# A clustered-attention and feed-forward kernel: the last unit's two output tiles in two PSUM places, copied in halves by two engines, and another list of priority shifts

## The chip, the cores and the metric

The kernel runs on one core of one Trainium2 chip. The metric is the device time of one execution in microseconds. The kernel before takes 863.71 us, the median of 3 runs (863.14 to 864.28).

## The reference: what is computed

Sizes: 4 batches, 8 heads, 768 positions, head width 64; 16 clusters; a feed-forward net of 512 to 2048 to 512 on 3072 tokens. Cut to what matters:

```python
q_assign = argmax(einsum('bhsd,hcd->bhsc', q_n, c_n), -1)   # q_n, k_n, c_n: normalised rows
k_assign = argmax(einsum('bhsd,hcd->bhsc', k_n, c_n), -1)
scores = where(q_assign[..., :, None] == k_assign[..., None, :], q @ k.T / sqrt(D), -1e9)
attn = exp(scores - max) / sum
x = (attn @ v).transpose(0, 2, 1, 3).reshape(3072, 512)
h = x @ w_in                                   # 512 -> 2048
g = where(h >= 1, h, where(h <= -1, 0, (h + 1)**2 / 4))
out = g @ w_out                                # 2048 -> 512
```

Every position gets the label of the nearest centroid; attention runs only between equal labels; its result goes through the two-layer net.

## The kernel before

**The units.** The work is cut into 12 units u, one for each batch and each third of its 768 query positions (256 queries, `CQ`). A unit has four pairs of heads. For each pair come four score steps (`at_scores`): TensorE (PE) multiplies keys with queries into a PSUM place of two banks, `pair[0]` (page name `pair<-kv,q`), and VectorE (DVE) drains it with a custom operation into one of three SBUF buffers `sS`, with the row statistic in `sbi`; this drain is the operation that lets PE write the next scores. ScalarE (ACT) takes the exponential, ACT and GpSimd (POOL) split it into a high and a low f16 half (`hl`), and SyncE (SP) sends it through a transposing DMA (`pT<-hl`). `at_av` multiplies the transposed weights with the values into bank `banka`, and the result goes by way of `rb` to `x`. The labels of a batch's queries come from a small product with the centroids (`bankj<-cT,q`), whose operand `q` is a transposing DMA of the normalised queries `qn`.

**The net.** For each unit and each f of eight slices of the hidden width, `ffn1` does 24 matmuls into one of the banks `bankh`, `banki`, `bankj`; DVE, ACT and POOL make the activation `r` and its two halves `g`. `ffn2` then does 12 matmuls (`pair<-w,g`, 128x512) that add to `pair[1]`, which has two banks: one for each of the unit's two output tiles t (128 queries x 512). After the last f of a unit, ACT copies both tiles, with a scale, to the SBUF tile `o` (`o<-pair,f_io`, 128x512 each), and one DMA writes them out. For the last unit and the last f (`end`) the 12 matmuls come as six for tile 0 and then six for tile 1, and each tile has a DMA of its own. So `pair[0]` serves scores, `pair[1]` the output; in the first 22 steps (`EARLY`) scores use both in turn.

**The first 120 us** also load and prepare the weights (`w`, `wk`, `word`: operations of DVE, ACT and POOL on 128x1024 tiles), the queries and the keys of the first batch.

**What sets the order.** No engine instruction is issued where it stands in the code: `Recorder` records each with what it reads and writes. `issue` then plans: 59 passes (`BASE`) of list scheduling, forward and backward, with a price for each instruction; then each seed of the list `NUDGES` calls `nudge`, which draws from the seed some events (a run of neighbouring names, or every second or fifth) and shifts their priority by a random amount; and a last forward pass fixes one order for every engine. Line 350 of the kernel before, in `issue`, replays the recorded calls; so nearly all rows of the profile say L350, and the names of the tiles tell operations apart. An engine runs its own list strictly in order. `Recorder` also keeps two engines from touching the same PSUM bank at the same time.

Of the kernel before, what the change touches and what calls it, by code (L numbers as in the profile page):

```python
# [11 lines left out]
F32 = mybir.dt.float32  # L12
U32 = mybir.dt.uint32
AF = mybir.ActivationFunctionType
ALU = mybir.AluOpType
# [27 lines left out]
LOOK, MARGIN = 0.4, 4000  # L43
BASE = 59
NUDGES = (
# [25 lines left out]
)  # L71
TILED = 248

# [386 lines left out]
def view(buf, shape, dtype):  # L460
    n = 1
    for k in shape:
        n *= k
    ap = buf.bitcast(dtype)[:, :n]
    if len(shape) > 1:
        names = "abcd"[: len(shape)]
        ap = ap.rearrange(
            "p (" + " ".join(names) + ") -> p " + " ".join(names), **dict(zip(names[1:], shape[1:]))
        )
    return ap  # L470
# [3 lines left out]
def tile_clustered_attention_moe(  # L474
# [14 lines left out]
    DM, DFF = w_in.shape  # L489
# [5 lines left out]
    CT = 2  # L495
# [3 lines left out]
    NU = B * NCH  # L499
# [15 lines left out]
    rec = Recorder(tc)  # L515
# [7 lines left out]
    def new(tag, shape, dtype, n=1):  # L523

        if tag not in rings:
            size = mybir.dt.size(dtype)
            for k in shape:
                size *= k
            rings[tag] = Ring(tiles(tag, n, -(-size // 32) * 32))
        return rings[tag](*shape, dtype=dtype)  # L530
# [23 lines left out]
    pair = [psum.tile([P, 1024], F32, name=f"pair{i}") for i in range(2)]  # L554
# [617 lines left out]
    F = {}  # L1172
# [27 lines left out]
    def ffn2(u, f):  # L1200
        b, c = divmod(u, NCH)
        e = FS[u, f]
        g = F.pop((u, f))
        if e["first"]:
            F[u] = view(pair[1], [CT, DM], F32)
        po = F[u]
        terms = [(s, i, *x) for s in range(2) for i, x in enumerate(((0, 0), (0, 1), (1, 0)))]
        end = u == NU - 1 and f == NF - 1

        parts = [(terms, [t]) for t in range(CT)] if end else [(terms[:3], range(CT)), (terms[3:], range(CT))]  # L1210
        for part, ts in parts:
            with rec.group():
                for s, i, ga, wa in part:
                    for t in ts:
                        rec.tensor.matmul(
                            po[:, t],
                            g[:, ga, s * CQ + t * P : s * CQ + (t + 1) * P],
                            w2[f][:, wa, s, :],
                            start=(e["first"] and s == 0 and i == 0),
                            stop=(e["last"] and s == 1 and i == 2),  # L1220
                        )
        if e["last"]:
            fresh = (u, "o") not in F
            if fresh:
                F[u, "o"] = new("o", [CT, DM], F32)
            ob = F[u, "o"]
            for t in range(CT):
                if fresh:
                    rec.scalar.activation(out=ob[:, t], in_=po[:, t], func=AF.Copy, scale=e["io"])
                else:  # L1230
                    rec.vector.scalar_tensor_tensor(
                        out=ob[:, t], in0=po[:, t], scalar=e["io"], in1=ob[:, t], op0=ALU.mult, op1=ALU.add
                    )
        if f == NF - 1:
            to = out.rearrange("(b p t) e -> b p t e", b=B, t=T)[b, :, c * CT : (c + 1) * CT, :]
            for part in [slice(t, t + 1) for t in range(CT)] if end else [slice(0, CT)]:
                rec.sync.dma_start(to[:, part], ob[:, part])
# [14 lines left out]
    for b in range(B):  # L1252
# [11 lines left out]
        for c in range(NCH):  # L1264
            u = b * NCH + c
            s0 = first(b, 0, c)
            for x, fn in zip((PRO, -9.1, -8.1, -6.1) if u == 0 else (s0 - 14, s0 - 6.8, s0 - 6.4, s0 - 4.5), (q_load, q_scale, q_split, q_assign)):
                at(x, fn, u)
            for hp in range(0, NP, NP if c else 1):
                at(first(b, hp, c) - (5.5 if u == 0 else 3), q_pairs, u, hp, NP if c else 1)  # L1270
            for hp in range(NP):
                s0 = first(b, hp, c)
                for n in range(SC):
                    at(s0 + n, at_scores, b, hp, c, n // CT, n % CT)
                    at(s0 + n + 1, at_soft, b, hp, c, n // CT, n % CT)
                at(s0 + LA - 0.5, at_av, b, hp, c)

            sf = max(sf, s0 + FA)
            G = NF if u else GF
            for f in range(NF):  # L1280
                if f % G == 0 and (u < 2 or c == 0):
                    if u == 0:
                        sf = max(sf, wat[2 * (f + G) - 1] + 2)
                    at(sf - 1, ffn_scale, [u] if u == 0 else range(u, (b + 1) * NCH), range(f, f + G))
                at(sf, ffn1, u, f)
                at(sf + 3, ffn2, u, f)
                sf += 2
# [50 lines left out]
```

## Time and profile before

| | |
|---|---|
| time, median of 3 runs | 863.71 us |
| the profiled execution's own time | 860.89 us |
| its span, first to last instruction | 859.1 us |
| mean granted TensorE clock | 0.985 |
| busy: PE, DVE, ACT, POOL | 802.4, 652.3, 639.1, 548.3 us |
| DMA | 142.53 MB, mean 166 GB/s |

The profile is one execution. Its span lacks 1.8 us that lie around the first and the last instruction, and it is 2.8 us below the median of the runs. Rows of groups give busy time, the mean of one instruction, and the idle time of the engine just before them with what ended it; rows of a timeline give start, length, engine, line, operation, tiles and count, and in brackets the idle time before and its releaser. PE's rows overlap a little, because matmuls are pipelined.

### The profile page before, as it was taken

How to read it: one execution, taken by the hardware profiler on the slowest of the kernel's cores; microseconds unless marked ns; L12 is line 12 of the kernel's file. 1: busy time of each engine (PE TensorE's matmuls, PEld its weight loads, DVE VectorE, ACT ScalarE, POOL GpSimd, SP SyncE). 2: the span in 40 equal slices, each digit the busy share in tenths (PEclk: the TensorE clock that was granted, in tenths of full speed). 3: DMA queues.
4: the chain of work that ended last, by engine and by line, in shares of the span. 5: the costliest groups of instructions: out<-in, count | busy, mean ns of one | idle time of the engine just before them, and what ended most of it. 6: DMA issues, size and time to landing. Idle time of an engine off the chain costs nothing.

```text
span 859.1 us, 19058 instructions
## 1 busy us (share of the span) xinstructions
PE 802.4 (93%) x7148; PEld 555.1 (65%) x7148; DVE 652.3 (76%) x1507; ACT 639.1 (74%) x1128; POOL 548.3 (64%) x527
## 2 busy tenths in 40 slices
PE   3677669999999999999999999999999999999997
PEld 2555446576666776767676766766676767676664
DVE  7999999989977877678888768678888767544322
ACT  6889898897877787687776787786876686776232
POOL 1156887887666768676766678656667567766221
PEclk9989899999999999999999999999999999999999
DMA  9975799889999989999898989997998696755100
GB/s 305 253 218 136 231 208 193 161 156 195 208 167 166 191 144 175 192 183 181 174 223 137 176 149 174 195 188 172 188 181 165 124 174 122 121 124 114 20 26 25
DMA packets 404766, 142.53 MB, mean 166 GB/s; under 512 B 372800, under 2 KB 396352, under 8 KB 404672
## 3 DMA queue, kind: packets, MB, share of 16 engines
q1 hardware_dynamic: 404672, 141.30, 81.7%
q8 instruction: 56, 0.92, 0.4%
q14 instruction: 38, 0.31, 0.1%
HBM read 40.40 MB, written 6.29 MB: 54 GB/s over the span
## 4 chain that ended last, share of the span: by engine, by line
PE 71%; DVE 9%; issue 3%; ACT 3%; POOL 3%; DMA 2%; ACTq 0%; DVEq 0%; POOLq 0%
PE pair L350 35%; PE banka L350 10%; PE banki L350 9%; PE bankj L350 9%; PE bankh L350 8%; DVE sS L350 2%; DVE r L350 2%; DMA q<-qn 1%; POOL hl L350 1%; ACT sS L350 1%; DVE qn L350 1%; DMA pT<-hl 1%; ACT hl L350 1%; DVE w L350 1%; DVE banki L350 0%
## 5 line engine op out<-in xcount | busy, mean ns | idle before, releaser
L350 POOL TENSOR_TENSOR hl<-sS,hl 128x768 f16<-128x768 f32 x176 | 297.4, 1695 | 109.6 <-ACT hl L350 90.4
L350 PE MATMUL pair<-w,g 128*128 128x512 f16 x1152 | 272.9, 380 | 0.7 <-ACT o L350 0.7
L350 PEld LDWEIGHTS <-w 128*128 128x128 f16 x2304 | 223.9, 98 | 50.3 <-issue 5.7
L350 ACT ACTIVATE sS<-sS,sbi 128x768 f32<-128x768 f32 x192 | 179.2, 933 | 86.7 <-DVE sbi L350 80.6
L350 DVE CUSTOM_DVE_ANT_0 sS<-pair,zero,er 128x768 f32<-128x768 f32 x192 | 193.8, 1011 | 48.3 <-PE pair L350 43.2
L350 PEld LDWEIGHTS <-g 128*128 128x128 f16 x1152 | 110.8, 98 | 116.1 <-issue 3.6
L350 PE MATMUL pair<-kv,q 128*128 128x384 f16 x768 | 158.3, 329 | 17.1 <-ACT pT L350 8.5
L350 POOL TENSOR_TENSOR g<-r,g 128x512 f16<-128x512 f32 x88 | 106.4, 1209 | 74.3 <-ACT g L350 64.1
L350 ACT CAST hl<-sS 128x768 f16<-128x768 f32 x176 | 144.0, 825 | 9.7 <-DMA pT<-hl 6.6
L350 PEld LDWEIGHTS <-q 128*128 128x128 f16 x992 | 78.7, 98 | 72.3 <-issue 25.5
L350 PE MATMUL banka<-pT,kv 128*64 128x256 f16 (+1 forms) x1680 | 106.3, 280 | 0.2 <-DMA pT<-hl 0.2
L350 ACT ACTIVATE r<-r,f_ra,f_rs 128x512 f32<-128x512 f32 x88 | 71.2, 809 | 37.5 <-DVE r L350 35.1
L350 PEld LDWEIGHTS <-kv 128*64 128x64 f16 (+1 forms) x1824 | 92.4, 108 | 4.0 <-ACT kv L350 1.4
L350 ACT CAST g<-r 128x512 f16<-128x512 f32 x88 | 53.8, 612 | 16.9 <-DVE r L350 8.0
L350 PE MATMUL bankj<-x,w 128*128 128x256 f16 x408 | 48.6, 272 | 3.4 <-POOL x L350 1.8
L350 PE MATMUL bankh<-x,w 128*128 128x256 f16 x432 | 51.8, 273 | 0.0
L350 POOL TENSOR_TENSOR qn<-qn,phi 128x256 f16<-128x256 f16 x48 | 33.0, 704 | 16.1 <-DVE phi L350 11.0
L350 POOL TENSOR_TENSOR w<-w 128x1024 f16<-128x1024 f32 x12 | 28.8, 2409 | 16.1 <-ACT w L350 16.1
L350 PE MATMUL banki<-x,w 128*128 128x256 f16 x312 | 37.7, 273 | 0.1
L350 PE MATMUL banki<-wk,w 128*128 128x256 f16 x312 | 37.4, 273 | 0.0
L350 ACT ACTIVATION_READ_ACCUMULATOR sS<-sS,sbi 128x1 f32 x192 | 36.0, 187 | 0.0
L350 DVE TENSOR_SCALAR r<-bankh,f_lo,f_hi 128x512 f32<-128x512 f32 x30 | 24.2, 805 | 13.7 <-PE bankh L350 10.9
(252 smaller groups left out, 1068.0 us busy)
## 6 DMA issues: line engine op xcount, KB each, us to landing
w<-in_moe_w_out_dram SPq DMA_DIRECT2D x14, 512.0 KB, 5.2
q<-in_q_dram SPq DMA_DIRECT2D x12, 512.0 KB, 4.7
kv<-in_k_dram SPq DMA_DIRECT2D x16, 384.0 KB, 4.3
kv<-in_v_dram SPq DMA_DIRECT2D x16, 384.0 KB, 4.1
out_dram<-o SPq DMA_DIRECT2D x11, 512.0 KB, 3.4
w<-in_moe_w_in_dram SPq DMA_DIRECT2D x10, 512.0 KB, 6.9
word<-in_moe_w_in_dram SPq DMA_DIRECT2D x6, 512.0 KB, 4.6
o<-in_v_dram SPq DMA_DIRECT2D x8, 384.0 KB, 3.9
```

The lines of the kernel that those rows point to most:

```text
L350: fn(*args, **kw)
```

## The change

`ffn2` holds a unit's output as a list of two views instead of one. For units 0 to 10 these are the two banks of `pair[1]` as before. For the last unit, tile 1 goes to the first bank of `pair[0]`. At the end of the last unit each tile is copied in two halves, columns 0 to 255 by ACT and columns 256 to 511 by DVE, where one ACT instruction copied 512 columns. And `NUDGES` is another list: 158 seeds from 1650000017 to 1650094381 stand for 194 seeds from 1700000017 to 1700116959. The rules of `nudge` are the same. The seeds are arguments to a hash, so their values say nothing to a reader; one line of each list is shown.

```diff
 NUDGES = (
-    1700000017, 1700000018, 1700000028, 1700000071, 1700000073, 1700000079, 1700000104, 1700000109,
...
+    1650000017, 1650000027, 1650000052, 1650000066, 1650000181, 1650000212, 1650000275, 1650000278,
...
         if e["first"]:
-            F[u] = view(pair[1], [CT, DM], F32)
+            F[u] = [pair[1][:, t * DM : (t + 1) * DM] for t in range(CT)]
+            if u == NU - 1:
+                F[u][1] = pair[0][:, :DM]
         po = F[u]
...
                         rec.tensor.matmul(
-                            po[:, t],
+                            po[t],
...
             for t in range(CT):
-                if fresh:
-                    rec.scalar.activation(out=ob[:, t], in_=po[:, t], func=AF.Copy, scale=e["io"])
+                if end:
+                    half = DM // 2
+                    rec.scalar.activation(out=ob[:, t, :half], in_=po[t][:, :half], func=AF.Copy, scale=e["io"])
+                    rec.vector.tensor_scalar(
+                        out=ob[:, t, half:], in0=po[t][:, half:], scalar1=e["io"], scalar2=None, op0=ALU.mult
+                    )
+                elif fresh:
+                    rec.scalar.activation(out=ob[:, t], in_=po[t], func=AF.Copy, scale=e["io"])
```

PE, ACT, POOL and SP have as many recorded instructions as before; DVE has two more, the two halves. The orders are the same but for small swaps up to about 100 us of the profile before; from there on all five differ. Three places follow. Numbers behind the names tell buffers apart (`pair0_79` is `pair[0]`).

**The end, ACT and DVE.** The last rows of ACT before, with the semaphores that they wait for:

```order
L350 ACTIVATE hl1_172<-hl1_172,f_ra0_194,f_rs0_199 128x512 [waits DVE_49]
L350 CAST g1_76<-hl1_172 128x512 [waits DVE_49,PE_49,Pool_49]
L350 ACTIVATE o0_68<-pair1_80,f_io0_189 128x512 [waits DMAHW0_49,PE_49]
L350 ACTIVATE o0_68<-pair1_80,f_io0_189 128x512
L1333 UNCONDITIONAL_BRANCH
```

The last rows of ACT now:

```order
L345 ACTIVATE hl1_172<-hl1_172,f_ra0_194,f_rs0_199 128x512 [waits DVE_49]
L345 CAST g1_76<-hl1_172 128x512 [waits DVE_49,PE_49,Pool_49]
L345 ACTIVATE o0_68<-pair1_80,f_io0_189 128x256 [waits DMAHW0_49,PE_49]
L345 ACTIVATE o0_68<-pair0_79,f_io0_189 128x256 [waits PE_49]
L1336 UNCONDITIONAL_BRANCH
```

The last rows of DVE now:

```order
L345 SCALAR_TENSOR_TENSOR hl0_171<-banki_83,f_gs0_204,hl0_171 128x512 [waits Activation_49]
L345 TENSOR_SCALAR hl1_172<-bankj_84,f_lo0_184,f_hi0_179 128x512 [waits PE_49,Pool_49]
L345 SCALAR_TENSOR_TENSOR hl1_172<-bankj_84,f_gs0_204,hl1_172 128x512 [waits Activation_49]
L345 TENSOR_SCALAR o0_68<-pair1_80,f_io0_189 128x256 [waits DMAHW0_49,Activation_49]
L345 TENSOR_SCALAR o0_68<-pair0_79,f_io0_189 128x256 [waits Activation_49]
L1336 UNCONDITIONAL_BRANCH
```

ACT's two copies are half as wide and each has a wait for PE of its own; DVE's halves stand at the end of its list and wait for ACT, not for PE: a tile's two halves follow one another. SP's two output DMAs wait for DVE now, for ACT before.

**PE behind the preparation of the last weights (about 116 to 124 us of the profile before).** PE before; `wk,ones` is part of the weight preparation, `kv1,q1` and `kv2,q1` are scores of unit 1, `w0,g0` is ffn2 of unit 0, `idu,rr` and `pT,kv` belong to `at_av`; repeats are left out:

```order
L350 MATMUL bankj_84<-aq0_126,ones_113 128x4
...
L350 MATMUL bankh_82<-wk0_69,ones_113 128x128
...
L350 MATMUL pair0_79<-kv1_62,q1_66 128x384
...
L350 MATMUL pair1_80<-w0_78,g0_75 128x512
...
L350 MATMUL banka_81<-idu_93,rr1_168 64x128
...
L350 MATMUL banka_81<-pT2_166,kv0_61 64x256
```

PE now:

```order
L345 MATMUL bankj_84<-aq0_126,ones_113 128x4
...
L345 MATMUL bankh_82<-wk0_69,ones_113 128x128
...
L345 MATMUL pair0_79<-kv1_62,q1_66 128x384
...
L345 MATMUL pair0_79<-kv2_63,q1_66 128x384
...
L345 MATMUL banka_81<-idu_93,rr1_168 64x128
...
L345 MATMUL banka_81<-pT2_166,kv0_61 64x256
```

Six ffn2 matmuls that stood between a score group and `at_av` have moved to behind the `at_av` group, and the next score group stands in their place, directly behind the score that uses the same PSUM place.

**DVE, the rescaling of the queries of batch 1 for the next head pair (about 136 to 141 us).** `ISA` is the drain of the scores. DVE before:

```order
L350 ISA sS0_85,sbi2_158<-pair0_79,zero_111,er1_148 128x768
L350 ISA sbi2_158 128x1
L350 TENSOR_REDUCE v_am1_125<-x2_74 128x1
L350 TENSOR_TENSOR banki_83<-zs0_145,mx0_146 128x16x16
L350 ISA sS1_86,sbi3_159<-pair0_79,zero_111,er1_148 128x768
L350 ISA sbi3_159 128x1
L350 TENSOR_TENSOR banki_83<-banki_83,iota_94 128x16x16
L350 TENSOR_REDUCE mx0_146<-banki_83 128x16
L350 TENSOR_TENSOR zs0_145<-banki_83,mx0_146 128x256
L350 TENSOR_SCALAR q1_66<-q1_66,phi0_149 128x512
```

DVE now:

```order
L345 ISA sS0_85,sbi2_158<-pair0_79,zero_111,er1_148 128x768
L345 ISA sbi2_158 128x1
L345 TENSOR_SCALAR q1_66<-q1_66,phi0_149 128x512
L345 TENSOR_REDUCE zs0_145<-banki_83 128x256
L345 SCALAR_TENSOR_TENSOR r0_209<-bankh_82,f_gs0_204,r0_209 128x512
L345 TENSOR_REDUCE mx0_146<-zs0_145 128x16
L345 ISA sS1_86,sbi3_159<-pair0_79,zero_111,er1_148 128x768
```

The rescaling `q1<-q1,phi` stood behind the drain into `sbi3` and three operations more; it now stands ahead of that drain.

Further on, on PE: the ffn1 group that starts at 157.85 us before now has an `at_av` group of 36 matmuls ahead of it; the ffn2 group that starts at 165.09 us has 33 matmuls between it and the `at_av` group ahead of it, where 16 stood, and ACT's two copies of unit 0's tiles to `o`, which had three operations between them, now follow each other directly behind the copy `rb<-banka` of that `at_av` group; and the label group `bankj<-cT,q` of unit 3, which stood between an `at_av` group and a score, now stands between two score groups, with nothing else between these.

More of the change, by code (lines that the diff above doesn't have):

```diff
@@ L1227, in ffn2 @@
             for t in range(CT):
-                if fresh:
-                    rec.scalar.activation(out=ob[:, t], in_=po[:, t], func=AF.Copy, scale=e["io"])
+                if end:
[6 more added lines that the diff above has]
+                    rec.scalar.activation(out=ob[:, t], in_=po[t], func=AF.Copy, scale=e["io"])
                 else:
                     rec.vector.scalar_tensor_tensor(
-                        out=ob[:, t], in0=po[:, t], scalar=e["io"], in1=ob[:, t], op0=ALU.mult, op1=ALU.add
+                        out=ob[:, t], in0=po[t], scalar=e["io"], in1=ob[:, t], op0=ALU.mult, op1=ALU.add
                     )
```

43 rows, old and new, of the table NUDGES are left out of this document.

## The prediction

> **What bounds the kernel now.** I read the page first (busy times, the slices, the chain), then the windows, then PE's waits, then the timeline at each of them.
>
> ```profile
> PE 802.4 (93%) x7148; PEld 555.1 (65%) x7148; DVE 652.3 (76%) x1507; ACT 639.1 (74%) x1128; POOL 548.3 (64%) x527
> ...
> PE   3677669999999999999999999999999999999997
> DVE  7999999989977877678888768678888767544322
> PEclk9989899999999999999999999999999999999999
> ...
> PE 71%; DVE 9%; issue 3%; ACT 3%; POOL 3%; DMA 2%; ACTq 0%; DVEq 0%; POOLq 0%
> ```
>
> PE carries 93% of the span and 71% of the chain that ended last. The slices show where it is not full: the first six, about 120 us, in which DVE has the 9s. The windows put numbers to that:
>
> ```profile
> 20.00:120.00 100.00, 69.07 (x616) 49.47 (x612) 97.97 (x233) 91.24 (x139) 58.74 (x45) 0.90 0.79 213
> ...
> 0.00:120.00 120.00, 74.67 (x705) 54.38 (x706) 112.47 (x277) 103.94 (x159) 61.88 (x72) 0.91 0.81 227
> 120.00:854.60 734.60, 727.75 (x6444) 500.71 (x6442) 539.79 (x1231) 533.85 (x968) 486.39 (x456) 1.00 0.83 156
> ```
>
> From 20 to 120 us DVE is busy for 97.97 of 100 us; up to 120 us PE idles 120 − 74.67 = 45.33 us. Behind that PE idles only 734.60 − 727.75 = 6.85 us in 734.6, at a granted clock of 1.00. The change leaves every PE instruction as it is, so from 120 us on an order can win at most these 6.85 us, and what lies behind the last matmul. PE's waits from 120 us on name them:
>
> ```profile
> PE pair L350 <- DVE sbi L350: 4.1, 4, 2.9
> PE bankj L350 <- DMA q<-qn: 1.2, 2, 1.0
> PE bankj L350 <- DVE r L350: 1.0, 2, 0.6
> PE pair L350 <- DVE q L350: 0.8, 1, 0.8
> PE bankj L350 <- DVE has L350: 0.8, 1, 0.8
> PE pair L350 <- ACT o L350: 0.7, 1, 0.7
> PE bankj L350 <- DVE f_rs L350: 0.6, 1, 0.6
> PE banka L350 <- DMA pT<-hl: 0.2, 1, 0.2
> ```
>
> They sum to 9.4 us; the longest, 2.9, ends at 119.74 us and lies ahead of the window, so 6.5 us of 6.85 are named. A measurement of this kernel can tell about 0.2%, 1.7 us, from no change: a quarter of that budget.
>
> **The end.** Last matmuls, ACT's two copies, the two DMAs; then the rows that price a half.
>
> ```profile
> 851.62 2.97 PE L350 MATMUL pair<-w,g 128*128 128x512 f16 x13
> 854.63 1.26 ACT L350 ACTIVATE o<-pair,f_io 128x512 f32<-128x512 f32 x2 [4.53 <-PE pair L350]
> 855.35 0.91 SPq L350 DMA_DIRECT2D out_dram<-o  x2
> ...
> L350 ACT ACTIVATE o<-pair,f_io x24: 665/679/687, 162.1 to 855.2; 128x512 f32<-128x512 f32 x24
> ...
> L350 PE MATMUL pair<-w,g 128*128 128x512 f16 x1152 | 272.9, 380 | 0.7 <-ACT o L350 0.7
> ...
> L350 ACT CAST g<-r 128x512 f16<-128x512 f32 x88 | 53.8, 612 | 16.9 <-DVE r L350 8.0
> ...
> L350 ACT COPY rb<-banka x48: 345/360/374, 54.4 to 802.5; 128x256 f32<-128x256 f32 x48
> L350 DVE TENSOR_TENSOR rb<-banka,rb x44: 393/419/426, 133.8 to 802.9; 128x256 f32<-128x256 f32 x44
> ...
> L350 ACT CAST x<-rb x24: 387/402/441, 58.9 to 685.0; 128x256 f16<-128x256 f32 x24
> ...
> out_dram<-o SPq DMA_DIRECT2D x2, 256.0 KB, 2.1
> ```
>
> PE ends at 854.59 and both copies lie behind that, though tile 0's six matmuls are over 6 x (2.97 − 0.38)/12 = 1.3 us earlier: the copy of tile 0 waits for all of the tile `pair[1]`. They end at 854.63 + 1.26 = 855.89. With tile 1 in `pair[0]`, tile 0 is copied from about 853.3, beside tile 1's matmuls, and its DMA leaves at about 854.3. Behind PE stands one tile. ACT's half: a cast is 612 ns at 512 columns and 402 at 256, 0.21 less, so 0.68 − 0.21 = 0.47 us; DVE's half 0.42 (`rb<-banka,rb`, as wide, out of PSUM too), estimates both. The order lets DVE wait for ACT, so they add: 854.63 + 0.47 + 0.04 + 0.45 = 855.59, or −0.30. The first DMA, now 1 us ahead, leaves the second more of the 2.1 us that they share: 0 to −0.2. I take −0.45; the bounds are −0.3 and, if the halves lay side by side, −0.95.
>
> On that I weighed the Trainium skill: its page "PSUM — Partial Sum Buffer", section "PSUM bank collisions raise a hardware error", says that two engines must not touch one bank in the same quadrant at the same time. By it the cut into halves can bring no overlap, only the shorter second operation; no run here shows two engines in one bank at once.
>
> **The new order, up to 120 us.** DVE sets this stretch, its work is the same and stands there in the same order but for swaps of single operations. A swap moves a drain by one operation, such as the 0.80 us of an `r` (first row below), and back again. I take 0, bounds −0.8 and +0.8.
>
> **The new order, 119 to 127 us.**
>
> ```profile
> L350 DVE TENSOR_SCALAR r<-bankh,f_lo,f_hi 128x512 f32<-128x512 f32 x30 | 24.2, 805 | 13.7 <-PE bankh L350 10.9
> ...
> 119.74 1.44 PE L350 MATMUL pair<-kv,q 128*128 128x384 f16 x4 [2.90 <-DVE sbi L350]
> 120.97 2.44 PE L350 MATMUL pair<-w,g 128*128 128x512 f16 x6
> ...
> 124.05 2.15 PE L350 MATMUL banka<-pT,kv 128*64 128x256 f16 x35 [0.19 <-DMA pT<-hl]
> ...
> 126.60 1.46 PE L350 MATMUL pair<-w,g 128*128 128x512 f16 x6
> ...
> 121.98 1.00 DVE L350 CUSTOM_DVE_ANT_0 sS<-pair,zero,er 128x768 f32<-128x768 f32 x1
> 122.92 0.08 DVE L350 DVE_READ_ACCUMULATOR2_ANT sbi<- 128x1 f32 x1
> ```
>
> Before, six ffn2 matmuls fill the time from the score at 119.74 until `pT` lands at 124.05; at that place they take 2.44 us where the same six take 1.46 at 126.60, so PE runs at about half speed behind its wait of 2.90 us, and at full speed again in the `at_av` row. Now a score stands in their place and must wait until the score before is drained, by this row until about 123.0, less 0.7 as one such `r` has left DVE's list ahead of it: 122.3. PE then idles about 1.2 us, does the score and is ready for `at_av` by about 123.9 (0.25 us of transposes included), when `pT` lands anyway. What is lost is that 2.44 us of slow ffn2 are left for later, where they take 1.3 (1.46 less the overlap of its last matmul), while a score of 0.65 to 1.2 us is done already. With a clock that is full again by then, 1.3 − 0.65 less what goes of the 0.19 and of the slow work: +0.35. With a clock that stays at half through the `at_av` group, whose 2.15 us become 4.3, +2.5. I take +1.0, nearer the first, since the idle time is shorter than the 2.90 that went with the slow rows.
>
> The Trainium skill, "TensorE: Matmul & The Clock Gate", Part 1, says that the clock falls to half after an idle window of about 3.4 us and is full again after a busy one; by that rule a new idle stretch inside the slow window would keep it slow, which is the slower case below. The rows agree on the half speed (1.44 us for a score here).
>
> **The new order, 127 to 167 us.**
>
> ```profile
> 133.94 0.81 PE L350 MATMUL pair<-kv,q 128*128 128x384 f16 x4 [0.20 <-DVE sbi L350]
> ...
> 141.53 0.82 PE L350 MATMUL pair<-kv,q 128*128 128x384 f16 x4 [0.82 <-DVE q L350]
> ...
> 157.85 1.47 PE L350 MATMUL bankj<-x,w 128*128 128x256 f16 x12 [0.64 <-DVE f_rs L350]
> ...
> 165.09 1.46 PE L350 MATMUL pair<-w,g 128*128 128x512 f16 x6 [0.75 <-ACT o L350]
> ```
>
> Four waits, 2.41 us, whose causes the order moves. The rescaling of `q1` stands one drain and three operations earlier on DVE, more than 0.82. The `f_rs` group has an `at_av` group of 2.15 us ahead of it, more than 0.64. The last: between that `at_av` group and ffn2 PE has 33 matmuls, at the spacing of these rows (0.11 for 256 columns, 0.16 for 384) about 3.9 us, and ACT has 0.36 + 2 x 0.68 = 1.7. All gone: −2.4. At least the first of the three large ones goes: −0.8.
>
> **The new order, behind 167 us.**
>
> ```profile
> L350 DVE SCALAR_TENSOR_TENSOR qn<-q,sq,qn x4: 470/474/1283, 181.9 to 184.7; 128x256 f16<-128x256 f32 x4
> ...
> 190.23 0.57 PE L350 MATMUL bankj<-cT,q 128*128 128x32 f16 x16 [0.22 <-DMA q<-qn]
> 190.65 0.81 PE L350 MATMUL pair<-kv,q 128*128 128x384 f16 x4
> ```
>
> The label group now stands between two scores of one PSUM place. It fills 0.42 us (190.23 to 190.65); the drain that the second score needs is 1.08. That is +0.7 at least; and the distance from `qn` to the label is, by the order, about 1.1 us of PE work shorter, of which 0.22 was waited for before: +1.3 at most, as both waits overlap. I take +1.0. Scores with less than 1.4 us of PE work between them are ten now, five before; a drain can come up to 1.15 us late there (by the order, some 2.5 us of DVE's operations between two drains, an estimate from such rows, against 1.35 of PE's). For this +0.5, bounds 0 and +1.2. The 3.9 us of later waits (6.5 − 2.41 − 0.19) lie where the orders differ through and through; I let them stand, and their bounds are −3.9 and +2.
>
> **The sum.** −0.45 + 0 + 1.0 − 2.4 + 1.0 + 0.5 = −0.35 us against the profiled 860.89, which is 860.5; the runs' median is 2.8 us above the profiled one, and the same step from 863.71 gives 863.3.
>
> **Rivals.** *Faster:* the new waits don't come, because the operations that they wait for move too: −0.45 + 0.35 − 2.4 = −2.5, or 861.2; with all the later waits gone as well −6.4, 857.3. For it: waits of 0.2 to 0.9 us are of the size of single operations. Against: a label group between two scores is in the list, whatever else moves. 0.35. *Slower:* half clock through the `at_av` group at 124 us. It decides when the new idle stretch at 121 us falls into the time in which the clock comes back. Then +2.5 instead of +1.0, and all behind it is 1.5 us later; with only 0.8 of the four waits gone, −0.45 + 2.5 − 0.8 + 1.5 = +2.75, or 866.5. For it: the two rows at half speed stand directly ahead. 0.24. *The change does not what it says:* the halves do not run together by the order; were they to, the end would give −0.95 and the sum −0.85, still no change that can be told.
>
> **The numbers.** My forecast, no change that can be told, has 0.41; its own range is 862.0 to 865.4. The faster case has 0.35 and the slower 0.24. The range for 8 in 10 reaches into both: from 859.6 (the faster case and 1.6 us of the later waits) to 866.8, just over the slower case.
>
> **What would show it.** In the profile after: the first `o<-pair` of the end beside PE's last six matmuls, the last tile copied by 855.6 on the time scale of before (1.0 us behind PE's end, not 1.3); no wait for `q`, `f_rs` and `o` between 127 and 167 us; a wait for `sbi` of about 1.2 us near 121, and the speed of the `at_av` row behind it (2.15 or 4.3); a wait for `sbi` or `q<-qn` by the label group. PE's idle time from 120 us to its end should stay within 2 us of 6.85. I am wrong if that sum is under 4 or over 9, or if PE's idle time up to 120 us moves by over 0.8 from 45.33.

## The result, and the profile after

| | before | after |
|---|---|---|
| time, median of the runs | 863.39 us (6 runs, 862.69 to 864.28) | 870.37 us (6 runs, 868.65 to 873.21) |
| ratio to before, 95% interval | | 1.009 (1.0068 to 1.0112) |
| the profiled execution: time, span | 860.89, 859.1 us | 870.75, 869.0 us |

The kernel became 7.0 us slower; the range ended at 866.8. One execution of the new end alone (below) took 2110 us; its ratio leaves that one out. The page of the kernel after, busy times and slices:

```profile
PE 805.8 (93%) x7148; PEld 555.6 (64%) x7148; DVE 668.7 (77%) x1509; ACT 635.7 (73%) x1128; POOL 540.2 (62%) x527
...
PE   3676669999999999999999999999999999999998
...
PEclk9989779999999999999999999999999999999999
```

What looks different is early: PE's fourth slice, 65 to 87 us (6, was 7), and the clock's fifth and sixth, 87 to 130 us (77, was 89). DVE is busy 16.4 us longer with two short operations more. The windows after, to 120 us and from there to the last matmul:

```profile
0.00:120.00 120.00, 76.20 (x696) 53.28 (x697) 112.19 (x270) 98.35 (x150) 52.79 (x68) 0.90 0.78 219
120.00:864.60 744.60, 729.27 (x6452) 502.29 (x6451) 555.98 (x1239) 536.89 (x978) 487.38 (x459) 0.99 0.82 155
```

PE's idle time up to 120 us is 43.8 us (45.33 before); behind that it is 15.33 (6.85). So the new idle time, 8.5 us, is behind 120 us; PE is also busy for 1.5 us more on either side of it, with as many matmuls in all. PE around there, after:

```profile
112.42 2.78 PE L345 MATMUL banki<-x,w 128*128 128x256 f16 x24
116.12 0.81 PE L345 MATMUL pair<-kv,q 128*128 128x384 f16 x4 [0.91 <-DVE sbi L345]
119.67 0.16 PE L345 MATMUL bankj<-aq,ones 128*128 128x4 bf16 x1 [2.75 <-DVE r L345]
120.27 0.62 PE L345 MATMUL bankh<-wk,ones 128*128 128x128 bf16 x8 [0.44 <-DVE wk L345]
124.12 1.44 PE L345 MATMUL pair<-kv,q 128*128 128x384 f16 x4 [3.23 <-DVE sbi L345]
126.78 1.44 PE L345 MATMUL pair<-kv,q 128*128 128x384 f16 x4 [1.23 <-DVE sbi L345]
128.15 0.64 PE L345 MATMUL banka<-idu,rr 128*64 128x128 f16 x8
128.58 3.46 PE L345 MATMUL banka<-pT,kv 128*64 128x256 f16 x36
```

The same place before:

```profile
112.32 0.81 PE L350 MATMUL pair<-kv,q 128*128 128x384 f16 x4 [1.26 <-DVE sbi L350]
112.97 2.78 PE L350 MATMUL banki<-x,w 128*128 128x256 f16 x24
116.22 0.62 PE L350 MATMUL bankh<-wk,ones 128*128 128x128 bf16 x8 [0.44 <-DVE wk L350]
```

From 116.9 to 124.1 us PE now waits 2.75 + 0.44 + 3.23 = 6.4 us, where it waited 0.44 + 2.90 = 3.3 before. Two scores then take 1.44 us, where a score takes 0.81 at a full clock (before, one score took 1.44), and the `at_av` group takes 3.46 instead of 2.15. In the kernel before, the `banki` group of 24 stood behind the corresponding score and shortened that gap; now it is done ahead of it. PE's later waits, after (single rows of the timeline; there are six more of 0.3 to 0.9 us):

```profile
252.79 0.81 PE L345 MATMUL pair<-kv,q 128*128 128x384 f16 x4 [0.86 <-DVE sbi L345]
427.34 0.81 PE L345 MATMUL pair<-kv,q 128*128 128x384 f16 x4 [0.93 <-DVE sbi L345]
484.04 1.14 PE L345 MATMUL bankj<-word,w 128*128 128x256 f16 x9 [2.09 <-DVE zs L345]
523.83 0.81 PE L345 MATMUL pair<-kv,q 128*128 128x384 f16 x4 [0.82 <-DVE sbi L345]
586.94 1.45 PE L345 MATMUL pair<-w,g 128*128 128x512 f16 x6 [1.47 <-ACT o L345]
```

What stands ahead of the longest, on DVE:

```profile
479.21 1.87 DVE L345 TENSOR_TENSOR bankj<-zs,mx 128x256 f32<-128x256 f32 x1
481.00 1.73 DVE L345 TENSOR_SCALAR q<-q,phi 128x512 f16<-128x512 f16 x1
482.65 0.42 DVE L345 TENSOR_TENSOR bankj<-bankj,iota 128x256 f32<-128x256 f32 x1
```

On POOL at the same time:

```profile
479.10 5.12 POOL L345 TENSOR_TENSOR hl<-sS,hl 128x768 f16<-128x768 f32 x3
```

And one row of the view of the tile `q`, least, median and greatest length in ns:

```profile
L345 DVE TENSOR_SCALAR q<-q,phi x48: 333/348/2215, 21.9 to 736.3; 128x512 f16<-128x512 f16 x48
```

POOL does three operations of 1.7 us without a break; two DVE operations that start in them take 1.87 and 1.73 us, where `q<-q,phi` has a median of 348 ns and the third, which takes one of its inputs from PSUM, 0.42. PE waits for what comes behind them on DVE.

The end, after:

```profile
856.96 7.93 PE L345 MATMUL pair<-w,g 128*128 128x512 f16 x36
...
863.63 0.48 ACT L345 ACTIVATE o<-pair,f_io 128x256 f32<-128x256 f32 x1 [3.23 <-PE pair L345]
864.14 0.48 DVE L345 TENSOR_SCALAR o<-pair,f_io 128x256 f32<-128x256 f32 x1 [4.47 <-ACT o L345]
864.65 1.63 SPq L345 DMA_DIRECT2D out_dram<-o  x2
864.93 0.47 ACT L345 ACTIVATE o<-pair,f_io 128x256 f32<-128x256 f32 x1 [0.82 <-PE pair L345]
865.43 0.48 DVE L345 TENSOR_SCALAR o<-pair,f_io 128x256 f32<-128x256 f32 x1 [0.81 <-ACT o L345]
```

Tile 0 is copied beside tile 1's matmuls; the last copy ends at 865.91, 1.02 us behind PE's last matmul (864.89), where it was 1.30; the span ends 4.1 us behind it, where it was 4.5.

### The profile page after: what moved, and what is told of

Read it like the earlier page. It is cut to its first block, busy times and chain, and to the rows that moved or that the text cites. A ratio compares the mean times of both kernels' runs of the same rounds, so it can differ in the third digit from the quotient of the medians.

```text
span 869.0 us, 19074 instructions
## 1 busy us (share of the span) xinstructions
PE 805.8 (93%) x7148; PEld 555.6 (64%) x7148; DVE 668.7 (77%) x1509; ACT 635.7 (73%) x1128; POOL 540.2 (62%) x527
## 4 chain that ended last, share of the span: by engine, by line
PE 67%; DVE 13%; issue 3%; ACT 2%; DMA 2%; POOL 2%; SPq 0%; DVEq 0%; POOLq 0%; ACTq 0%
PE pair L345 33%; PE banka L345 10%; PE bankh L345 9%; PE banki L345 8%; PE bankj L345 8%; DVE sS L345 3%; DVE r L345 2%; POOL hl L345 1%; DMA pT<-hl 1%; DVE qn L345 1%; DVE bankj L345 1%; DVE banki L345 1%; DVE w L345 1%; ACT sS L345 1%; DMA q<-qn 1%
## 5 line engine op out<-in xcount | busy, mean ns | idle before, releaser
L345 PE MATMUL pair<-kv,q 128*128 128x384 f16 x768 | 163.3, 338 | 19.9 <-DVE sbi L345 11.2
L345 PEld LDWEIGHTS <-q 128*128 128x128 f16 x992 | 80.9, 100 | 76.9 <-issue 33.9
L345 PEld LDWEIGHTS <-ones 128*128 128x128 bf16 x256 | 18.3, 105 | 26.7 <-issue 20.8
```

What stands on the lines that cost most here:

```text
L345: fn(*args, **kw)
```

## The experiments

Most kernels below don't plan: they replay a written-out order, so that each engine's list is known. Kernels with no other word replay the list of the kernel before or after, row by row. Where a diff makes an order out of another, or moves an operation, the kernel holds the order that comes of it. Ratios are to the kernel before, run beside them, with 95% intervals.

```diff
-        prio = {x: x.step for x in self.nodes}
-        for _ in range(BASE):
...
-        self.forward(prio)
         with self.tc.manual_schedule():
-            for x in self.order:
+            for i in order:
+                x = self.nodes[i]
                 for fn, args, kw in x.calls:
                     fn(*args, **kw)
```

### The end or the order

**The new end alone** (the change's edits to `ffn2`, the order of before).

> The kernel before, its own order on every engine, with the new end alone (tile 1 of the last unit in pair[0], copies in halves). If the list of shifts made the loss: faster than before by about 0.4 us (0.3 to 0.95), which is within the 0.2% that can be told. If the new end makes the loss (the last unit's second tile in the place of the scores, or DVE's halves late): slower by most of 7 us.

Measured: 862.65 us, 0.9994 (0.9979 to 1.0008). No change that can be told.

**The new order alone** (the end of before, the order of after).

> The kernel after, its own order on every engine, with the old end (both tiles in pair[1], one ACT copy of 512 columns each). If the order makes the loss: about 7 us slower than before, 0.4 slower than the changed kernel. If the new end makes it: within 1 us of before.

Measured: 870.54 us, 1.009 (1.0072 to 1.0108). The order makes the whole loss.

**The list of shifts left out** (the kernel after, planned as before).

```diff
-NUDGES = (
...
+NUDGES = ()
```

> The changed kernel with an empty list of shifts: the order that the 59 passes give by themselves. If the new list made a good order worse by what the price model does not know: faster than the changed kernel. If each list is a draw: anywhere between 860 and 880 us; my guess from the two lists is 868, 5 us slower than before.

Measured: 871.41 us, 1.0102 (1.0081 to 1.0124). The new list is worth about 1 us against none, less than the intervals can tell; the old one was worth 8. So the change did not spoil an order: it gave up a list that was worth 8 us on the chip for one that is worth next to nothing there.

### Where in the order

**The new order up to about 153 us, then the old**, and **the old, then the new**; old end in both.

```diff
-order = new
+early = [i for i in new if planned_start[i] < 150]
+order = early + [i for i in old if i not in early]    # and with old and new exchanged
```

> The order of the changed kernel for all that it starts up to about 153 us, from there on the order of the kernel before; old end. In the two traces the changed kernel has done the same amount of matmul work 4.8 us later at that point and 10.3 us later at the end. If each stretch costs what it shows there: about 4 to 5 us slower than before. If the early lag is only work that is put off and caught up: no change. If all later lag follows from the early one: about 7 us.

> The other way round: the order of the kernel before up to about 153 us, then that of the changed kernel; old end. If each stretch costs what it shows: 2.5 to 5.5 us slower than before, and the two stretches add up to about 7 to 8. If all comes from the early stretch: no change.

Measured: 867.85 us, 1.0061 (1.0041 to 1.0081), and 872.81 us, 1.0103 (1.0086 to 1.012). The early stretch costs about 5 us, a wait at the seam included: 2.06 us, where the kernel before waits 0.64 for `f_rs` and the kernel after not at all.

```profile
163.05 1.47 PE L385 MATMUL bankj<-x,w 128*128 128x256 f16 x12 [2.06 <-DVE f_rs L385]
```

The second misses: 2.5 to 5.5 us were expected, and it is no faster than the whole new order. At its seam, too, stands a wait that no other kernel has:

```profile
164.14 3.00 PE L385 MATMUL banka<-pT,kv 128*64 128x256 f16 x35 [3.33 <-DMA pT<-hl]
```

So the two do not add up, and the price of the later stretch is not to be had from this pair. It is read better from one window, 140 to 850 us, of the kernel before, the new end alone, the kernel after and the new order alone; the first number behind the length is PE's busy time:

```profile
140.00:850.00 710.00, 703.55 (x6262) 486.23 (x6261) 521.62 (x1196) 517.10 (x941) 471.03 (x444) 1.00 0.83 155
```

```profile
140.00:850.00 710.00, 703.34 (x6261) 486.07 (x6260) 522.71 (x1199) 516.99 (x940) 471.21 (x445) 1.00 0.82 155
```

```profile
140.00:850.00 710.00, 699.39 (x6245) 483.51 (x6244) 531.80 (x1201) 513.79 (x940) 467.37 (x448) 1.00 0.83 157
```

```profile
140.00:850.00 710.00, 699.51 (x6221) 483.35 (x6221) 533.61 (x1200) 513.71 (x940) 466.52 (x447) 1.00 0.82 156
```

PE idles 6.5 and 6.7 us there in the old order, 10.6 and 10.5 in the new: +4 us, and at the same places. The new order alone has them again, in another run:

```profile
253.65 0.81 PE L385 MATMUL pair<-kv,q 128*128 128x384 f16 x4 [0.83 <-DVE sbi L385]
428.18 0.81 PE L385 MATMUL pair<-kv,q 128*128 128x384 f16 x4 [0.93 <-DVE sbi L385]
484.54 0.70 PE L385 MATMUL bankj<-word,w 128*128 128x256 f16 x4 [2.02 <-DVE zs L385]
```

### PE's clock in the early stretch

PE does some matmuls again in its idle time, into the places where they stand already.

```diff
+FILL = {554: (611, 612), 578: (578,) * 7}    # after; before: {578: (578,) * 6}
...
-                for fn, args, kw in x.calls:
-                    fn(*args, **kw)
+                for j in (i, *FILL.get(i, ())):
+                    for fn, args, kw in self.nodes[j].calls:
+                        fn(*args, **kw)
```

> The changed kernel in its own order; PE does some matmuls again in its idle time between 116 and 124 us (24 of an ffn1 group once, 8 of the weight preparation seven times, to the same places with the same values), which nothing waits for. In the trace of the changed kernel the granted clock is 0.50 to 0.63 from 120 to 132 us and the at_av group there takes 3.46 us, before 2.15. If half clock behind the idle time is a part of the loss: clock 1.0 there, at_av 2.15, and 2 to 3.5 us faster than the changed kernel, so 4 to 5.5 slower than before. If DVE sets this stretch whatever the clock: no gain.

> The same in the kernel before: the 8 matmuls of the weight preparation seven times in all, in the idle time of 2.9 us that ends at 119.7. Half clock lasts only about 3 us there: 0 to 1 us faster than before by the clock, no change if DVE sets the stretch.

Measured: 867.76 us, 1.005 (1.0032 to 1.0067), and 862.64 us, 0.9989 (0.9976 to 1.0002). The window from 120 to 132 us of the kernel before, of the new end alone, of the kernel after, then of the kernel after with the repeats, the granted clock third from the end; last, the `at_av` group with the repeats:

```profile
120.00:132.00 12.00, 11.81 (x101) 7.57 (x100) 10.21 (x20) 9.93 (x16) 6.28 (x5) 0.88 1.13 213
```

```profile
120.00:132.00 12.00, 10.15 (x98) 6.97 (x98) 11.96 (x22) 9.98 (x17) 6.95 (x5) 1.00 1.11 216
```

```profile
120.00:132.00 12.00, 7.27 (x61) 4.64 (x61) 11.96 (x19) 12.00 (x22) 11.34 (x6) 0.57 1.14 227
```

```profile
120.00:132.00 12.00, 9.49 (x112) 6.90 (x110) 11.61 (x20) 10.98 (x21) 10.93 (x7) 1.00 1.11 217
```

```profile
125.66 2.52 PE L387 MATMUL banka<-pT,kv 128*64 128x256 f16 x36
```

Matmuls that compute nothing new bring the clock from 0.57 to 1.00, the `at_av` group from 3.46 to 2.52 us and the kernel from 7 to 8 us behind to 4.2: keeping PE busy there wins back about 3 us. In the old order, where the window shows 0.88 (profile of before) or 1.00 (new end alone), the same gains nothing that can be told.

Not all of the 3 us is shown to be the half clock itself. Ahead of the first repeat the trace with repeats is 2.1 us ahead of that of the kernel after and 0.2 behind that of the new order alone (the same score starts at 109.64, 111.78 and 109.41 us). At the ffn1 group of 12 behind the stretch it is 1.8 and 1.9 ahead (152.84; 154.62 and 154.76), at the end 5.0 and 6.4 (spans of 864.0; 869.0 and 870.4). So by one pair of traces the early stretch wins about 2 us, by the other nothing, and in both 3 to 4.5 us come later, where the lists are the same. There the wait of 2.09 us is missing, that near 587 us is 0.20 instead of 1.47, and PE idles 8.2 us from 140 to 850 us instead of 10.6. DVE's operation that took 1.87 us ahead of the longest wait takes 0.42, in a pause of POOL:

```profile
140.00:850.00 710.00, 701.80 (x6257) 485.62 (x6255) 533.08 (x1199) 513.46 (x939) 468.00 (x448) 1.00 0.81 156
```

```profile
478.15 0.42 DVE L387 TENSOR_TENSOR bankj<-zs,mx 128x256 f32<-128x256 f32 x1
```

```profile
476.43 1.65 POOL L387 TENSOR_TENSOR hl<-sS,hl 128x768 f16<-128x768 f32 x1
479.88 3.30 POOL L387 TENSOR_TENSOR hl<-sS,hl 128x768 f16<-128x768 f32 x2 [1.80 <-ACT hl L387]
```

So the later waits are not fixed by the lists alone: they also hang on which operations of DVE and POOL happen to meet.

### DVE's waits for POOL

POOL's subtractions of 256 columns and more as two instructions of half the width, in both orders.

```diff
+                    if x.eng == "gpsimd" and kw.get("op") == ALU.subtract and len(kw["out"].shape) == 2 and kw["out"].shape[1] >= 256:
+                        n = kw["out"].shape[1] // 2
+                        for a in (slice(0, n), slice(n, 2 * n)):
+                            fn(out=kw["out"][:, a], in0=kw["in0"][:, a], in1=kw["in1"][:, a], op=ALU.subtract)
+                        continue
```

> The kernel before in its own order, but each of POOL's subtractions of 256 columns and more is done as two instructions of half the width. In the traces DVE's operations on SBUF alone take longer than their least time only while POOL works (in all 51 us before, 71 after). If such a DVE operation waits for the end of POOL's running instruction, halves halve the wait: DVE's excess falls from about 51 to 25 to 30 us, and the time by 1 to 3 us. If the two share a bandwidth, or the excess has another cause: excess as before, and the time up by 0 to 2 us, since POOL has some 290 starts more.

> The same cut of POOL's subtractions in the changed kernel with its own order. If DVE's waits for POOL make the loss: DVE's excess falls from about 71 to 35 to 45 us, and the kernel is 2 to 4 us slower than the kernel before instead of 7 to 8. If the loss lies in the order's dependences: 7 us slower still.

Measured: 864.01 us, 1.0005 (0.9994 to 1.0016), and 869.37 us, 1.0056 (1.0044 to 1.0068). The 51 and 71 us of the expectation count every row against the shortest tenth of its kind; no page shows that count. The page's busy times, with the same number of operations, put the two kernels 16.4 us apart, not 20. With halves, in the old order and in the new:

```profile
PE 806.2 (94%) x7148; PEld 556.7 (65%) x7148; DVE 656.3 (76%) x1507; ACT 640.5 (74%) x1128; POOL 602.0 (70%) x863
```

```profile
PE 808.4 (93%) x7148; PEld 557.0 (64%) x7148; DVE 658.5 (76%) x1509; ACT 636.5 (73%) x1128; POOL 601.7 (69%) x863
```

DVE falls from 668.7 to 658.5 us in the new order, but not in the old (652.3 to 656.3): halves do not halve the waits. With DVE now 2 us apart between the orders, the kernels are still 5.4 us apart; against the kernel before, the new order is 4.8 us behind, between the two outcomes expected. So DVE's longer time is for the most part not the loss.

**POOL writes zeros there** and reads nothing.

```diff
-                    fn(*args, **kw)
+                    self.nc.gpsimd.memset(kw["out"], 0.0)    # for POOL's subtractions of 256 columns and more
```

> The kernel before in its own order; POOL's subtractions of 256 columns and more are left out and POOL writes zeros to the same places, so the low halves of the attention weights, the activations, x and the weights are zero (products to half precision). POOL then reads nothing from SBUF in these. If DVE waits for POOL: DVE's excess under 15 us, and 2 to 6 us faster than the kernel before. Otherwise excess and time much as before, but for what POOL's own steps cost on the path.

> The same with zeros in the changed kernel and its order. If DVE's waits for POOL make the loss: within 2 us of the kernel before with zeros. If the order's dependences make it: 5 us or more slower than that one.

Measured: 857.16 us, 0.9916 (0.9903 to 0.9928), and 860.73 us, 0.995 (0.9933 to 0.9966). DVE's busy time in the two:

```profile
PE 804.2 (94%) x7148; PEld 556.9 (65%) x7148; DVE 631.7 (74%) x1507; ACT 638.7 (75%) x1128; POOL 265.9 (31%) x527
```

```profile
PE 805.2 (94%) x7148; PEld 555.6 (65%) x7148; DVE 636.9 (74%) x1509; ACT 636.5 (74%) x1128; POOL 263.4 (31%) x527
```

DVE loses 21 and 32 us of busy time without a change of its own work, so that much hung on what POOL did. That is less than expected: 51 less 21 leaves 30 us of excess in the old order, not under 15. The orders are 3.6 us apart instead of 7 to 8: between the two outcomes expected. The zeros also halve POOL's time, so they shorten its own steps on the path as well; they do not tell the two apart.

**Four DVE operations of the new order moved** behind what PE waits for.

```diff
+move(407, after=555)    # q<-q,phi at 122 us, behind the drain
+move(632, after=610)    # two qn<-q,sq,qn, behind the third drain
+move(634, after=632)
+move(2298, after=2265)  # q<-q,phi at 481 us, behind the labels
```

> The changed kernel with four of DVE's operations on SBUF moved behind the operation that PE waits for: at about 122 us one q<-q,phi (1.45 us in the trace, 0.34 alone) behind the next drain, and two qn<-q,sq,qn (0.92 and 1.17, alone 0.48) behind the third drain; at about 481 us one q<-q,phi (1.73 us) behind the labels for which PE waits 2.09 us. All other engines keep their order. If DVE's waits for POOL ahead of what PE waits for make the loss: the wait of 2.09 us falls under 0.6, that near 126 us by about 1 us, and the kernel is 2 to 3 us faster than the changed kernel, so 4.5 to 5.5 slower than before. If such a wait only moves to another operation: no gain.

Measured: 870.64 us, 1.0098 (1.0079 to 1.0118). No gain, though the wait at the labels falls from 2.09 to 0.58:

```profile
483.02 2.78 PE L385 MATMUL bankj<-word,w 128*128 128x256 f16 x24 [0.58 <-DVE zs L385]
490.91 0.50 PE L385 MATMUL pair<-kv,q 128*128 128x384 f16 x2 [1.06 <-DMA q<-qn]
```

8 us later PE waits 1.06 us for the queries `q`, for which it did not wait in the kernel after. The wait near 126 us stays at 1.23. The drain ahead of it starts at 120.61 us, where it starts at 120.69 in the trace of the new order alone: with `q<-q,phi` out of the way, it waits for POOL instead.

```profile
120.61 1.02 DVE L385 CUSTOM_DVE_ANT_0 sS<-pair,zero,er 128x768 f32<-128x768 f32 x1 [1.25 <-POOL hl L385]
```

Between this drain and the next the moved `q<-q,phi`, 0.77 us, stands in the place of the `qn` of 0.92 that was moved away. So moving single DVE operations gains nothing; the rival, that such a wait moves on, is what this run shows.

**Halves and filling together.**

> The changed kernel with both at once: PE kept busy in its idle time at 116 to 124 us, and POOL's subtractions in halves. Alone the first left 4.2 us of the loss of 7 to 8, the second 4.9. If they are two causes that add up: 1 to 2.5 us slower than before. If they are one cause (the halves only help because they bring the clock back, or the other way round): 4 to 5 us slower, as each alone.

Measured: 868.48 us, 1.0051 (1.0037 to 1.0066), 4.5 us slower than before, as each alone: the two do not add up. In its trace the clock is 0.86 from 120 to 132 us, not 1.00, and PE idles 11.0 us from 140 to 850 us; of its later waits several are new. So this run does not tell whether the two are one cause.

### A faster version

**The order of before, the new end, five DVE operations moved**, then the same **with PE kept busy**.

```diff
+move(409, before=670)   # q<-q,phi near 141 us, ahead
+move(733, after=764)    # q<-q,phi near 156, behind f_rs
+move(2303, after=2315)  # qn<-zs near 472, behind the drain
+move(3101, after=3078)  # q<-q,phi near 645, behind has
+move(2737, before=2797) # r near 576, ahead
```

> The kernel before with the new end and five of DVE's operations moved: behind what PE waits for a q<-q,phi of 1.54 us near 156 (PE waits 0.64 for f_rs), a qn<-zs of 1.73 near 472 (0.53 for sbi) and a q<-q,phi of 1.84 near 645 (0.75 for has); ahead of other work the q<-q,phi near 141 (0.82 for q) and an r near 576 (0.35 for r). If PE's waits behind 120 us can be had one by one: 3.1 us and 0.4 at the end, so 3 to 3.5 us faster than the kernel before. If moving them brings other waits: within 1 us of it.

> The kernel before with the new end, the five moved DVE operations and PE kept busy in its idle time before 119.7 us. Alone the first two together gave -1.3 us, the last -0.9 (interval from -2.1 to 0.2). If they add up: 2 to 2.5 us faster than before, the fastest of all. If not: about 1.3.

Measured: 861.48 us, 0.9985 (0.9971 to 0.9999), and 860.99 us, 0.9965 (0.9952 to 0.9978). The second is 3 us faster than the kernel before run beside it, the fastest here that leaves nothing out; that it is faster than the first, whose interval overlaps with its own, is not shown. The first gained 1.3 us by its ratio, less than half of the 3 to 3.5 that its waits promised: those for `q`, `f_rs` and `has` are gone, but a new one of 0.89 us stands at 145 us, and that for `o` at 166 us grew from 0.75 to 1.09:

```profile
144.65 0.62 PE L385 MATMUL bankj<-wk,ones 128*128 128x128 bf16 x8 [0.89 <-DVE wk L385]
165.93 1.46 PE L385 MATMUL pair<-w,g 128*128 128x512 f16 x6 [1.09 <-ACT o L385]
```

## Why the prediction was wrong

**What bounds the kernel: right.** PE idle behind 120 us was the budget, and its move from 6.85 to 15.33 us is most of the loss as the trace shows it; the prediction named over 9 as a sign of being wrong. Its other sign came too: PE's idle time up to 120 us moved by 1.5 us, where over 0.8 was named.

**The end, −0.45: right.** 1.02 us from PE's end to the last copy, as worked out, DVE's half behind ACT's, and 0.4 us less from PE's end to the span's. The new end alone, −0.06% with an interval of ±0.15%, does not contradict it; the bound of −0.95 for halves side by side is not what happens.

**Up to 120 us, 0: wrong where it mattered.** PE's idle time there moved by 1.5 us, to less, but the step looked at idle time alone. That the `banki` group had moved ahead of a score is in no term of the prediction. With that group done, 0.8 us of work is left to PE from 116.9 to 124.1 us. To put this group back by itself was not tried; what was tried is to repeat matmuls in its place.

**119 to 127 us, +1.0 taken, bounds +0.35 and +2.5: the failed step.** The wait worked out for the second score (1.2 us) is there, 1.23, but in part by luck: not only an `r` but also a `qn` left DVE's list between the two drains, and the `qn` that stayed took 0.92 us instead of 0.47. What failed is the clock, which the step let come back before the `at_av` group. It took the lower end because this idle time was shorter than the 2.90 us of before; but it came on top of 6.4 us of waits from 116.9 on. Half clock lasts into the `at_av` group, which takes 3.46 us (2.15 before, 4.3 in the slower rival, which had a chance of 0.24), and repeats in the idle time win back about 3 us of the kernel's time, of which the traces show up to 2 in this stretch. The whole early stretch, with the wait at its seam, measured +5 (new order up to 153 us: 0.41% to 0.81%). The page of the Trainium skill that the prediction named, "TensorE: Matmul & The Clock Gate", Part 1, has the clock at half after an idle window of about 3.4 us. The traces agree with the direction: 0.57 with 6.4 us of waits there, 1.00 once they are filled. The rule alone does not decide the case: no single wait here is that long (2.75 and 3.23), and a wait of 2.90 us went with 0.88 in the profile of before and with 1.00 in the new end alone. The price came from the run.

**127 to 167 us, −2.4: mis-sized.** The waits for `q` and `f_rs` are gone, as worked out. That for `o` is still 0.82, and new ones of 0.29 (`r`) and 0.93 us (`sbi`) stand between: −0.4 in all, short of the smallest gain allowed, −0.8. In the trace of the new order alone PE's waits in this stretch are 4.1 us, which is +1.7.

**Labels, +1.0, and scores close together, +0.5.** At the label place the rows show 0.63 and 0.86 where there were 0.48 and 0.22: +0.8. The later waits, which the prediction let stand at 3.9 us with a bound of +2, are 6.5 us from 200 us on, 3.3 more than before. Waits of 0.8 to 0.9 for `sbi` at 253, 427 and 524 us are 2.6 of them. Only the first stands between close scores; in the other two about 2.7 us of PE's work lie between the scores, so they, and the 2.09 for labels, were in no term. From 140 to 850 us PE idles 4 us more than before in the traces of the kernel after and of the new order alone, and 1.7 us more in that with repeats.

So the loss of 7 to 8 us is an early stretch of up to 5 us, in which the clock is at half, and waits of PE behind it, about 4 us in two traces. The two parts are not cleanly apart, since the kernel with repeats has fewer of the later waits as well. Why these stand where they do is not settled: POOL holds up DVE right ahead of the longest, and half of the gap between the orders goes when POOL's subtractions go; yet halves of them, or moving single operations, only move the waits. It was not tried to undo one close pair of scores at a time.

## What to carry to other kernels

Price a reordering by the gaps that it opens on the engine whose clock falls when it idles: add up all the waits in a row, not only the one that the moved work leaves. Here 6.4 us of waits were followed by half clock, and filling them won about 3 us. Waits of under 1 us that an order removes come back elsewhere in part (3.1 us removed by hand gave 1.3, and in the new order nothing), so a sum of removed waits was too much to expect in both. A list of seeds is worth what the chip says: here 8 us for the one, and for the other about 1, which the intervals do not tell from nothing.

## What the runs showed of the hardware

- DVE operations on SBUF alone can take longer while POOL works: `q<-q,phi` has a median of 348 ns and a maximum of 2215; with POOL's subtractions replaced by zeros DVE needs 21 to 32 us less for the same work.
- Repeating finished matmuls in PE's idle time can keep the clock full: with 80 more the granted clock from 120 to 132 us is 1.00 instead of 0.57, and the kernel after is about 3 us faster. Together with POOL's halves it was 0.86.
- One and the same wait of 2.90 us, behind the same list, went with a clock of 0.88 from 120 to 132 us in the profile of before and of 1.00 in that of the new end alone.
- The same order differs by a few us in the first 130 us from one execution to the next: in the run with the old order ahead of the seam, DVE drains the score that it drains at 121.98 us in the profile of before at 125.39, with the same list on every engine until then. One trace of this stretch cannot tell less than that: of the kernel after and of the new order alone, too, the same score starts at 111.78 and 109.41 us.
